# Band mask as a TensorE matmul, 18-token rows, a mode-contiguous spectrum and a pinned TensorE order in an attention and spectral-mix kernel

## Chip, cores and metric

The kernel runs on one core of a Trainium2 chip. The metric is the device time of one execution in microseconds, the median of several. The profile is of one execution; its times are counted from that execution's start.

## The reference

Eight batches of 576 tokens, 8 heads of 64. First comes attention in which a token sees itself and the 63 tokens before it; then a Fourier transform over the tokens, of which the first 64 modes are mixed, each by its own complex 512x512 matrix, transformed back and added; then one more matmul with a ReLU.

```python
def _attn_ref(q, k, v):                      # window = 64
    scores = scale * np.matmul(q, k.transpose(0, 1, 3, 2))
    rel = pos[:, None] - pos[None, :]
    scores = np.where((rel >= 0) & (rel < window), scores, -1e9)
    ...                                      # softmax over keys, times v
def _moe_ref(x, w_r, w_i, w_ch):
    X = np.fft.rfft(x, axis=1)               # first 64 modes, each with its own w_r, w_i (512x512)
    Yr = einsum('bmd,mde->bme', Xr, w_r) - einsum('bmd,mde->bme', Xi, w_i)
    Yi = einsum('bmd,mde->bme', Xr, w_i) + einsum('bmd,mde->bme', Xi, w_r)
    u = x + np.fft.irfft(Y, n=S, axis=1)
    return u + np.maximum(u @ w_ch, 0.0)
```

## The kernel before

The kernel has three stages. In stage 1, q, k and v of a batch are loaded and brought into place by TensorE (transposes of q and k, "pick" matmuls for v); attention then goes through 36 windows of 8 blocks of 64 tokens per head pair; the forward transform of each finished batch fills `XQ`. In stage 2 the 128 weight matrices (64 modes, real and imaginary) stream in and are multiplied with `XQ`. Stage 3 transforms back and writes the result. The program is written in an order, but where nothing else is said, a scheduler in the kernel language places the instructions of each engine.

These are the parts that the change touches (cuts marked `...`):

```python
RUN = S // 64                                            # 9 tokens per partition row
XQ = keep.tile([128, NC, NM, B, 3], BF16, name="XQ")     # mode outside, batch and part inside
ps_misc = ...tile_pool(name="ps_misc", bufs=2, space=PSUM)   # 2 buffers: transposes, v, transform
...
def main(src, dst, quad):                                # 4 such pieces per batch, 8 of 9 tokens
    def f():
        ps = ps_misc.tile([128, 8, 128], BF16, name="pst", tag="misc")
        for c in range(8):
            tr(src, quad, c, ps[:, c, :])
        evac(view(dst, quad * 2 * S, [[S, 2], [RUN, 64], [1, 8]]), view(ps, ...), 1024)
def last():                                              # the 9th token of each row, q and k
    ps = ps_misc.tile([128, 4, 128], BF16, name="psl", tag="misc")
    ...
    evac(view(dst, 8, [[S, 4], [RUN, 64]]), view(ps, ...), 256)     # single elements, 9 apart
def vpart(a, j0, j1):
    ...
    for c in range(4):
        for i in range(2):                               # two row groups, two PSUM tiles
            nc.tensor.matmul(out=pss[i][:, 0:n, :], lhsT=pick[pp, c, :], rhs=rv[pp, j0:j1, c, :], ...)
...
def scores(w):
    ...                                                  # 64x64 matmuls into pss[w % 2]
    nc.scalar.activation(out=et, in_=ps, func=ACT_F.Exp, scale=EX_SCALE)
    nc.vector.tensor_tensor(out=et, in0=et, in1=view(band, ...), op=ALU.mult)   # the band mask, 0 or 1
def weigh(w):
    for hh in range(2):
        for G in range(8 * w, 8 * w + 8):
            n, i = divmod(G, 9)                          # head, block of the head
            nc.tensor.matmul(out=pso[hh][...], lhsT=et[...], rhs=vt[...], start=True, stop=True)
            if i == 8:                                   # the head is complete: normalise it
                nc.vector.reciprocal(out=rcp, in_=view(pso[hh], D, ...))
                nc.vector.tensor_tensor(out=x_sb[...], in0=view(pso[hh], ...), in1=view(rcp, ...), op=ALU.mult)
def dft(b):
    ...
    nc.vector.tensor_copy(out=view(XQ, 3 * b + 1, [[NM * W3, NC], [1, 2], [W3, NM]]), in_=ps)
    nc.scalar.mul(out=view(XQ, 3 * b, [[NM * W3, NC], [W3, NM]]), in_=ps[:, :, 1, :], mul=-1.0)
...
for w in range(NWIN):                                    # 36 windows
    scores(w)
    for b, j in sched.get(w, []): units[b][j]()          # pieces of the next batch
    while dfts: dft(dfts.pop(0))
    if w: weigh(w - 1)
```

Note `pso[hh]`: each half `hh` has one PSUM buffer. The first block of the next head may write it only when the normalisation of the head before has read it.

The softmax here doesn't subtract the row's maximum and nothing guards it: scores larger than these inputs give would overflow.

## Time and profile before

| | kernel before |
|---|---|
| median time | 559.99 us (558.45 to 560.14) |
| stage 1, to the first spectral matmul | 216.7 us |
| stage 2, to the first inverse transform | 282.3 us |
| stage 3 | 60.0 us |

The first fence is the page's overview in 40 slices of 14 us: TensorE's busy tenths, the granted clock, the share of DMA and its GB/s.

```profile
PE   2988999988989777887888721222222222248882
...
PEclk9999999995665555799888855555555555559998
DMA  9999798979910020999999999999999999944554
GB/s 148 203 155 156 123 153 130 172 114 152 165 35 2 1 76 6 203 213 214 213 214 214 213 213 214 213 214 213 214 213 214 213 214 213 214 100 159 179 194 145
```

From slice 16 to 34 DMA runs at 203 to 214 GB/s, while TensorE, after some other work up to slice 22, is 10 to 20% busy: stage 2 is bounded by the weights. Just before it, slices 11 to 15, DMA is all but idle (the 76 GB/s of slice 14 are one other load), because every weight buffer is full and none comes free until stage 2 starts. So whatever shortens stage 1 shortens the whole.

Stage 1 in stretches of 20 us (window; then busy us and count for PE, PEld, DVE, ACT, POOL; granted clock; DMA share; GB/s):

```profile
60.00:80.00 20.00, 18.83 (x207) 11.36 (x206) 10.61 (x20) 10.63 (x14) 4.82 (x8) 1.00 0.86 131
80.00:100.00 20.00, 19.35 (x237) 12.40 (x235) 10.70 (x24) 12.23 (x14) 5.75 (x9) 1.00 0.91 144
100.00:120.00 20.00, 19.22 (x230) 12.12 (x229) 10.52 (x23) 10.27 (x14) 4.44 (x7) 1.00 0.78 133
160.00:180.00 20.00, 19.55 (x209) 11.70 (x207) 9.87 (x24) 9.30 (x14) 0.00 (x0) 0.50 0.00 1
```

TensorE is 94 to 98% busy in these stretches and about 80% in most others from 120 us on, so stage 1 is mainly TensorE's. The clock of 1.00 in the first three lines is not to be believed. The trace's first clock record is at 120 us, and the view takes full clock before it. The transforms tell otherwise: the chain of waits shows one of them at 79 us, 20 matmuls in 3.12 us, and within it the full-array matmuls of 128 columns start 107 ns apart; so they do at 58 and at 103 us. In a stretch of stage 2 where full clock is on record, 128-column transposes start 56 ns apart. Those are the two states, 1.2 and 2.4 GHz, of the Trainium skill, "TensorE: Matmul & The Clock Gate", Part 1. By this reading and the records from 120 us on, stage 1 ran at half clock except for 10 us of its 217.

The chain of waits at that transform (start, us, what):

```profile
79.11 3.12 PE psx L312 x20
82.26 2.50 DVE XQ L315
84.80 1.35 ACT XQ L316
```

The two copies into `XQ` follow one another and take 3.85 us together, and for that long they hold one of the two `ps_misc` buffers through which all pieces of the next batch pass.

The groups of stage 1 that the change touches (line, engine, operation, operands, shapes, count | busy us, mean ns | idle before, releaser):

```profile
L276 DVE TENSOR_TENSOR et<-et,band 128x1024 bf16<-128x1024 bf16 x36 | 24.8, 688 | 19.7 <-ACT et L274 19.6
...
L315 DVE CAST XQ<-psx 128x512 bf16<-128x512 f32 x8 | 20.0, 2504 | 16.9 <-PE psx L312 16.9
...
L316 ACT ACTIVATE XQ<-psx 128x256 bf16<-128x256 f32 x8 | 10.7, 1343 | 27.6 <-DVE XQ L315 16.1 <-DVE rcp L298 11.6
...
L62 ACT COPY qT<-pst 128x1024 bf16<-128x1024 bf16 x12 | 12.6, 1046 | 4.3 <-PE pst L206 3.9 <-PE pso_148 L291 0.4
L62 ACT COPY qT<-psl 128x256 bf16<-128x256 bf16 x5 | 7.8, 1564 | 1.5 <-DVE kT_142 L64 1.5
```

TensorE's waits for the normalisation, in stage 1 (who waited for whom: us, times, longest):

```profile
PE pso_148 L291 <- DVE x_sb L299: 4.3, 6, 1.5
...
PE pso_147 L291 <- DVE x_sb L299: 0.7, 1, 0.7
```

They are few: the scheduler puts other work between two heads.

### The profile page before, as it was taken

What the parts mean: (1) busy time and instruction counts of PE and PEld (TensorE: products, weight loads), DVE (VectorE), ACT (ScalarE), POOL (GpSimd) and SP (SyncE); (2) the same over time, 40 slices, a digit from 0 to 9 for tenths busy, and PEclk for the clock granted to TensorE, in tenths of its full rate; (3) what the DMA queues carried; (4) which work ended last, traced back from release to release, by engine and by line L of the source; (5) the groups of instructions that cost most, each with busy time, mean ns of one, the idle gap of its engine ahead of it and who ended that gap; (6) DMA issues with size and microseconds to landing.
All of it is one profiled execution on the core that took longest, in us unless ns stands there. A gap on an engine that the chain in (4) does not pass through costs nothing.

```text
span 559.0 us, 10870 instructions
## 1 busy us (share of the span) xinstructions
PE 354.5 (63%) x4760; PEld 242.7 (43%) x4760; DVE 188.8 (34%) x372; ACT 161.6 (29%) x226; POOL 156.5 (28%) x235
## 2 busy tenths in 40 slices
PE   2988999988989777887888721222222222248882
PEld 1655566555546546654555521222221222236551
DVE  4585555455545675523222200000000000016662
ACT  3468447553734622222222200000000000005552
POOL 8312133121300001312222212222122222009996
PEclk9999999995665555799888855555555555559998
DMA  9999798979910020999999999999999999944554
GB/s 148 203 155 156 123 153 130 172 114 152 165 35 2 1 76 6 203 213 214 213 214 214 213 213 214 213 214 213 214 213 214 213 214 213 214 100 159 179 194 145
DMA packets 42431, 92.45 MB, mean 165 GB/s; under 512 B 3472, under 2 KB 20880, under 8 KB 42384
## 3 DMA queue, kind: packets, MB, share of 16 engines
q0 software_dynamic: 37136, 82.32, 78.4%
q1 hardware_dynamic: 5248, 9.44, 4.8%
q8 instruction: 37, 0.61, 0.4%
q14 instruction: 10, 0.08, 0.0%
HBM read 163.58 MB, written 9.44 MB: 310 GB/s over the span
## 4 chain that ended last, share of the span: by engine, by line
DMA 40%; PE 24%; issue 16%; DVE 8%; POOL 6%; ACT 5%; POOLq 0%; DVEq 0%; ACTq 0%
DMA wt<-in_moe_w_r_dram 36%; POOL ot L478 5%; PE pst L206 4%; PE psx L312 3%; DMA wt<-in_moe_w_i_dram 3%; DVE XQ L315 3%; PE pso_148 L291 2%; PE pso_147 L291 2%; DVE u L474 2%; DMA rq<-in_q_dram 1%; PE pss_149 L269 1%; ACT qT L62 1%; ACT XQ L316 1%; PE pss_150 L269 1%; DVE qT L64 1%
## 5 line engine op out<-in xcount | busy, mean ns | idle before, releaser
L405 PE MATMUL psy<-XQ,wt 128*128 128x16 bf16 x1024 | 57.1, 174 | 86.6 <-DMA wt<-in_moe_w_i_dram 86.2
L402 PE MATMUL psy<-XQ,wt 128*128 128x16 bf16 x1024 | 59.6, 174 | 66.9 <-DMA wt<-in_moe_w_r_dram 63.4
L113 POOL DMA_DIRECT2D wt<-in_moe_w_r_dram x64 | 34.4, 538 | 222.8 <-PE psy L405 216.9
L405 PEld LDWEIGHTS <-wt 128*128 128x128 bf16 x1024 | 46.3, 102 | 92.9 <-DMA wt<-in_moe_w_i_dram 92.6
L402 PEld LDWEIGHTS <-wt 128*128 128x128 bf16 x1024 | 46.5, 103 | 79.4 <-DMA wt<-in_moe_w_r_dram 74.2
L408 DVE CAST YT<-psy 128x512 fp32r<-128x512 f32 x8 | 5.5, 691 | 180.5 <-PE psy L405 180.5
L478 POOL TENSOR_TENSOR ot<-u,r 128x512 f32<-128x512 f32 (+1 forms) x40 | 49.7, 1297 | 24.3 <-ACT r L476 24.3
L388 PE MATMUL psz<-wch,xT 128*128 128x512 f32 (+1 forms) x160 | 55.4, 472 | 1.8 <-DVE xT L385 1.4
L463 ACT CAST Yw<-psw_5958 128x512 fp32r<-128x512 f32 x1 | 0.6, 587 | 180.1 <-PE psw_5958 L458 180.1
L385 DVE CAST xT<-pxt 128x512 fp32r<-128x512 bf16 (+1 forms) x40 | 23.9, 632 | 65.9 <-PE pxt L382 65.9
L291 PEld LDWEIGHTS <-et 128*64 128x64 bf16 (+1 forms) x576 | 32.1, 146 | 31.6 <-issue 26.0
L390 ACT CAST Z_3076<-psz 128x512 fp32r<-128x512 f32 (+1 forms) x40 | 23.2, 583 | 70.3 <-PE psz L388 70.3
L113 POOL DMA_DIRECT2D wt<-in_moe_w_i_dram x64 | 35.1, 549 | 0.5 <-issue 0.5
L235 PEld LDWEIGHTS <-pick 32*128 32x128 bf16 x256 | 23.0, 121 | 25.9 <-issue 13.6
L388 PEld LDWEIGHTS psz<-wch,xT 128*128 128x128 f32 (+1 forms) x160 | 30.0, 209 | 7.7 <-ACT Z_3076 L390 2.4
L474 DVE TENSOR_TENSOR u<-psu,x_sb 128x512 f32<-128x512 f32 (+1 forms) x40 | 26.8, 688 | 19.5 <-POOL ot L478 13.3
L276 DVE TENSOR_TENSOR et<-et,band 128x1024 bf16<-128x1024 bf16 x36 | 24.8, 688 | 19.7 <-ACT et L274 19.6
L102 POOL DMA_DIRECT2D rv<-in_v_dram x32 | 19.5, 622 | 35.4 <-PE pss_149 L269 7.6
L476 ACT ACTIVATE r<-psc 128x512 f32<-128x512 f32 (+1 forms) x40 | 22.1, 598 | 22.8 <-PE psc L471 14.0
L315 DVE CAST XQ<-psx 128x512 bf16<-128x512 f32 x8 | 20.0, 2504 | 16.9 <-PE psx L312 16.9
L312 PE MATMUL psx<-trigF,x_sb 128*128 128x128 bf16 (+1 forms) x160 | 25.1, 303 | 0.0
L274 ACT ACTIVATE et<-pss_149 128x1024 bf16<-128x1024 f32 x18 | 19.5, 1081 | 14.0 <-PE pss_149 L269 13.2
(249 smaller groups left out, 613.4 us busy)
## 6 DMA issues: line engine op xcount, KB each, us to landing
wt<-in_moe_w_r_dram POOLq DMA_DIRECT2D x64, 512.0 KB, 16.1
wt<-in_moe_w_i_dram POOLq DMA_DIRECT2D x64, 512.0 KB, 18.0
out_dram<-ot SPq DMA_DIRECT2D x32, 256.0 KB, 2.0
rk<-in_k_dram POOLq DMA_DIRECT2D x8, 576.0 KB, 6.5
rq<-in_q_dram POOLq DMA_DIRECT2D x8, 576.0 KB, 7.4
rv<-in_v_dram POOLq DMA_DIRECT2D x32, 144.0 KB, 5.0
wch<-in_moe_w_ch_dram POOLq DMA_DIRECT2D x1, 1024.0 KB, 5.5
out_dram<-ot SPq DMA_DIRECT2D x8, 128.0 KB, 2.2
```

The costliest lines, as they stand in the source:

```text
L113: nc.gpsimd.dma_start(out=wt, in_=src[m].rearrange("(p c) e -> p c e", c=NC))
L276: nc.vector.tensor_tensor(out=et, in0=et, in1=view(band, 0, [[0, 2 * WIN // 128], [1, 128]]), op=ALU.mult)
L291: nc.tensor.matmul(out=pso[hh][po, (i // 2) * (D + 1):(i // 2 + 1) * (D + 1)], lhsT=et[pk, hh, col:col + 64], rhs=vt[pk, 1 - f % 2, 2 * qu ...
L312: nc.tensor.matmul(out=ps[:, c, :, :], lhsT=x_sb[:n, b, t, c:DM:NC], rhs=trigF[:n, t, :], start=(t == 0), stop=(t == NT - 1))
L315: nc.vector.tensor_copy(out=view(XQ, 3 * b + 1, [[NM * W3, NC], [1, 2], [W3, NM]]), in_=ps)
L385: nc.vector.tensor_copy(out=xT[:, :, 0:n], in_=pst[:, :, 0:n])
L388: nc.tensor.matmul(out=psz[:n, :], lhsT=xT[:, c, 0:n], rhs=wch[:, c, :], start=(c == 0), stop=(c == NC - 1))
L390: nc.scalar.copy(out=Z0[:n, b, t, :], in_=psz[:n, :])
L402: nc.tensor.matmul(out=psy[:, m % MG, e, :], lhsT=wr[:, c, ee], rhs=XQ[:, c, m, :, 1:3], start=(c == 0), stop=False)
L405: nc.tensor.matmul(out=psy[:, m % MG, e, :], lhsT=wi[:, c, ee], rhs=XQ[:, c, m, :, 0:2], start=False, stop=(c == NC - 1))
L474: nc.vector.tensor_tensor(out=u[:n, :], in0=psu[:n, :], in1=x_sb[:n, b, t, :], op=ALU.add)
L478: nc.gpsimd.tensor_tensor(out=ot[:n, :], in0=u[:n, :], in1=r[:n, :], op=ALU.add)
```

## The change

The intent is to take the mask off VectorE, to give TensorE more and wider work so that its clock rises, and to fix its order. The mask becomes a matmul: the identity times a band of 0 and -30000 opens the PSUM accumulation of each window, and the scores are added to it. Rows of 18 tokens per partition make six even transposing pieces per batch (3 for q, 3 for k), without the leftover. `XQ` gets the mode innermost, so its copies write contiguously. 24 warm-up matmuls go ahead. TensorE's instructions run in the order in which the program emits them, and the weighting of a window is cut into its two halves with pieces of the next batch between.

```diff
-    RUN = S // 64
+    RUN = S // 32
-    XQ = keep.tile([128, NC, NM, B, 3], BF16, name="XQ")
+    XQ = keep.tile([128, NC, B, 3, NM], BF16, name="XQ")
...
-        def main(src, dst, quad):  ...   # 8 chunks into PSUM, one copy of 1024
-        def last():  ...                 # the 9th token, two copies of 256, one for k and one for q
+        def part(src, dst, c0):
+            def f():
+                ps = ps_misc.tile([128, 6, 128], BF16, name="pst", tag="misc")
+                for c in range(6):
+                    for hh in range(2):
+                        nc.tensor.transpose(out=ps[64 * hh:64 * hh + 64, c, :], ...)
+                evac(view(dst, c0, [[S, 4], [RUN, 32], [1, 6]]), view(ps, ...), 768)
...
     def scores(w):
         ps = pss[w % 2]
+        for hh in range(2):
+            nc.tensor.matmul(out=ps[:, hh, :], lhsT=ident_bf, rhs=view(band, 0, [[0, WIN // 128], [1, 128]]),
+                             start=True, stop=False, skip_group_check=True)
...
-                                     start=True, stop=True, skip_group_check=True)
+                                     start=False, stop=True, skip_group_check=True)
-        nc.vector.tensor_tensor(out=et, in0=et, in1=view(band, ...), op=ALU.mult)
...
-    def weigh(w):
+    def weigh(w, hh):
...
-        nc.vector.tensor_copy(out=view(XQ, 3 * b + 1, [[NM * W3, NC], [1, 2], [W3, NM]]), in_=ps)
+        nc.vector.tensor_copy(out=view(XQ, b * 3 * NM + NM, [[BN, NC], [1, 2 * NM]]), in_=...)
...
+    with tc.manual_schedule(engines={mybir.EngineType.PE}):
+        warm_up(16)
...
+        for w in range(NWIN + 1):
+            todo = list(sched.get(w, []))
+            if w < NWIN: scores(w)
+            if todo: unit(*todo.pop(0))
+            if w: weigh(w - 1, 0)
+            if todo: unit(*todo.pop(0))
+            if w: weigh(w - 1, 1)
...
```

More of the change, by code (lines that the diff above doesn't have):

```diff
@@ L93, in load @@
     def load(b):
-        rk = rawp.tile([128, 4, RUN * D], BF16, name="rk")
-        rq = rawp.tile([128, 4, RUN * D], BF16, name="rq")
+        rk = rawp.tile([128, 2, RUN * D], BF16, name="rk")
+        rq = rawp.tile([128, 2, RUN * D], BF16, name="rq")
         rv = rawp.tile([128, 9, 4, D], BF16, name="rv")
@@ L98, in load @@
             nc.gpsimd.dma_start(
-                out=r, in_=src[b].rearrange("(x g) (p c) d -> (g p) x (c d)", g=2, c=RUN))
+                out=r, in_=src[b].rearrange("(x g) (p c) d -> (g p) x (c d)", g=4, c=RUN))
         vf = v[b].rearrange("(hp hl) t d -> hp (hl t) d", hl=2)
@@ L114, in load_w @@
         wtiles[i] = wt
+    warm = acons.tile([128, 512], BF16, name="warm")
+    nc.vector.memset(warm, 0.0)
     load(0)
@@ L130 @@
                                 base=0, pattern=[[-1, 4], [1, 128]], channel_multiplier=-4)
+    NEG = -30000.0
     band = acons.tile([128, 128], BF16, name="band")
-    nc.vector.memset(band, 1.0)
+    nc.vector.memset(band, 0.0)
     for half in range(2):
@@ L138 @@
         nxt_ = band[pp, 64 - 64 * half:128 - 64 * half]
-        nc.gpsimd.affine_select(out=own, in_=own, compare_op=ALU.is_ge, fill=0.0,
+        nc.gpsimd.affine_select(out=own, in_=own, compare_op=ALU.is_ge, fill=NEG,
                                 base=0, pattern=[[1, 64]], channel_multiplier=-1)
-        nc.gpsimd.affine_select(out=nxt_, in_=nxt_, compare_op=ALU.is_ge, fill=0.0,
+        nc.gpsimd.affine_select(out=nxt_, in_=nxt_, compare_op=ALU.is_ge, fill=NEG,
                                 base=-1, pattern=[[-1, 64]], channel_multiplier=1)
     load(1)
-    kTs = [acons.tile([128, 2, 2, S], BF16, name=f"kT{i}") for i in range(2)]
+    kTs = [acons.tile([128, 4, S], BF16, name=f"kT{i}") for i in range(2)]
     vts = [acons.tile([128, 2, 4, 9, D + 1], BF16, name=f"vt{i}") for i in range(2)]
@@ L154 @@
         nc.vector.memset(pso[i], 1.0)
-        nc.vector.memset(pss[i], 0.0)
     MAGIC = 12582912.0
@@ L199, in transpose_units @@
         rq, rk, rv = raws[b]
-        qT = qtp.tile([128, 2, 2, S], BF16, name="qT")
+        qT = qtp.tile([128, 4, S], BF16, name="qT")
         kT, vt = kTs[b % 2], vts[b % 2]
         qTs[b] = qT
-        def tr(src, quad, c, dst):
-            for hh in range(2):
-                nc.tensor.transpose(out=dst[64 * hh:64 * hh + 64, :],
-                                    in_=src[:, 2 * quad + hh, c * D:(c + 1) * D], identity=ident_bf)
-        def main(src, dst, quad):
-            def f():
-                ps = ps_misc.tile([128, 8, 128], BF16, name="pst", tag="misc")
-                for c in range(8):
-                    tr(src, quad, c, ps[:, c, :])
-                evac(view(dst, quad * 2 * S, [[S, 2], [RUN, 64], [1, 8]]),
-                     view(ps, 0, [[64, 2], [1, 64], [128, 8]]), 1024)
-            return f
-        def last():
-            ps = ps_misc.tile([128, 4, 128], BF16, name="psl", tag="misc")
-            for i, src in enumerate((rk, rq)):
-                for quad in range(2):
-                    tr(src, quad, 8, ps[:, 2 * i + quad, :])
-            for i, dst in enumerate((kT, qT)):
-                evac(view(dst, 8, [[S, 4], [RUN, 64]]),
-                     view(ps, 256 * i, [[64, 4], [1, 64]]), 256)
+        def part(src, dst, c0):
+            def f():
+                ps = ps_misc.tile([128, 6, 128], BF16, name="pst", tag="misc")
+                for c in range(6):
+                    for hh in range(2):
+                        nc.tensor.transpose(out=ps[64 * hh:64 * hh + 64, c, :],
+                                            in_=src[:, hh, (c0 + c) * D:(c0 + c + 1) * D],
+                                            identity=ident_bf)
+                evac(view(dst, c0, [[S, 4], [RUN, 32], [1, 6]]),
+                     view(ps, 0, [[32, 4], [1, 32], [128, 6]]), 768)
+            return f
         def vpart(a, j0, j1):
@@ L245, in vpart @@
             return f
-        return [main(rk, kT, 0), main(rq, qT, 0), last, vpart(0, 0, 5), vpart(0, 5, 9),
-                main(rk, kT, 1), main(rq, qT, 1), vpart(1, 0, 5), vpart(1, 5, 9)]
+        return [part(rk, kT, 0), part(rk, kT, 6), part(rk, kT, 12),
+                part(rq, qT, 0), part(rq, qT, 6), part(rq, qT, 12),
+                vpart(0, 0, 5), vpart(0, 5, 9), vpart(1, 0, 5), vpart(1, 5, 9)]
     def head_of(n):
-        return n // 4, n % 4 // 2, n % 2
+        return n // 4, n % 4
     def scores(w):
         ps = pss[w % 2]
+        for hh in range(2):
+            nc.tensor.matmul(out=ps[:, hh, :], lhsT=ident_bf, rhs=view(band, 0, [[0, WIN // 128], [1, 128]]),
+                             start=True, stop=False, skip_group_check=True)
         for G in range(8 * w, 8 * w + 8):
             n, blk = divmod(G, 9)
-            b, quad, g = head_of(n)
+            b, g = head_of(n)
             first = G == 8 * w
@@ L269, in scores @@
                     nc.tensor.matmul(out=ps[64 * half:64 * half + 64, hh, col:col + nq],
-                                     lhsT=kTs[b % 2][pp, quad, g, 64 * kb:64 * kb + 64],
-                                     rhs=qTs[b][pp, quad, g, q0:q0 + nq],
-                                     start=True, stop=True, skip_group_check=True)
+                                     lhsT=kTs[b % 2][pp, g, 64 * kb:64 * kb + 64],
+                                     rhs=qTs[b][pp, g, q0:q0 + nq],
+                                     start=False, stop=True, skip_group_check=True)
         et = etp.tile([128, 2, WIN], BF16, name="et")
@@ L275, in scores @@
         busy["ACT"] += 2 * WIN / 1.2 + 60
-        nc.vector.tensor_tensor(out=et, in0=et, in1=view(band, 0, [[0, 2 * WIN // 128], [1, 128]]), op=ALU.mult)
-        busy["DVE"] += 2 * WIN / 1.92 + 70
         ets[w] = et
-    def weigh(w):
-        et = ets.pop(w)
-        for hh in range(2):
-            for G in range(8 * w, 8 * w + 8):
-                n, i = divmod(G, 9)
-                b, quad, g = head_of(n)
-                vt = vts[b % 2]
-                f = G % 18
-                po = slice(64 * (i % 2), 64 * (i % 2) + 64)
-                col = 64 * (G - 8 * w)
-                pk = slice(0, 128) if i else slice(64 * (f % 2), 64 * (f % 2) + 64)
-                nc.tensor.matmul(out=pso[hh][po, (i // 2) * (D + 1):(i // 2 + 1) * (D + 1)],
-                                 lhsT=et[pk, hh, col:col + 64], rhs=vt[pk, 1 - f % 2, 2 * quad + hh, f // 2, :],
-                                 start=True, stop=True, skip_group_check=True)
-                if i == 8:
-                    ps = pso[hh]
-                    h = 4 * quad + 2 * hh + g
-                    rcp = small.tile([128, NT], FP32, name="rcp")
-                    nc.vector.reciprocal(out=rcp, in_=view(ps, D, [[D + 1, NT]]))
-                    nc.vector.tensor_tensor(
-                        out=x_sb[:, b, :, h * D:(h + 1) * D],
-                        in0=view(ps, 0, [[D + 1, NT], [1, D]]),
-                        in1=view(rcp, 0, [[1, NT], [0, D]]), op=ALU.mult)
-                    busy["DVE"] += NT * D / 0.96 + 150
-                    if h == H - 1:
-                        dfts.append(b)
@@ new lines, in weigh @@
+    def weigh(w, hh):
+        et = ets[w]
+        for G in range(8 * w, 8 * w + 8):
+            n, i = divmod(G, 9)
+            b, g = head_of(n)
+            vt = vts[b % 2]
+            f = G % 18
+            po = slice(64 * (i % 2), 64 * (i % 2) + 64)
+            col = 64 * (G - 8 * w)
+            pk = slice(0, 128) if i else slice(64 * (f % 2), 64 * (f % 2) + 64)
+            nc.tensor.matmul(out=pso[hh][po, (i // 2) * (D + 1):(i // 2 + 1) * (D + 1)],
+                             lhsT=et[pk, hh, col:col + 64], rhs=vt[pk, 1 - f % 2, 2 * hh + g // 2, f // 2, :],
+                             start=True, stop=True, skip_group_check=True)
+            if i == 8:
+                ps = pso[hh]
+                h = 4 * hh + g
+                rcp = small.tile([128, NT], FP32, name="rcp")
+                nc.vector.reciprocal(out=rcp, in_=view(ps, D, [[D + 1, NT]]))
+                nc.vector.tensor_tensor(
+                    out=x_sb[:, b, :, h * D:(h + 1) * D],
+                    in0=view(ps, 0, [[D + 1, NT], [1, D]]),
+                    in1=view(rcp, 0, [[1, NT], [0, D]]), op=ALU.mult)
+                busy["DVE"] += NT * D / 0.96 + 200
+                if h == H - 1:
+                    dfts.append(b)
@@ L313, in dft @@
                                  rhs=trigF[:n, t, :], start=(t == 0), stop=(t == NT - 1))
-        W3 = 3 * B
-        nc.vector.tensor_copy(out=view(XQ, 3 * b + 1, [[NM * W3, NC], [1, 2], [W3, NM]]), in_=ps)
-        nc.scalar.mul(out=view(XQ, 3 * b, [[NM * W3, NC], [W3, NM]]), in_=ps[:, :, 1, :], mul=-1.0)
+        BN = B * 3 * NM
+        nc.vector.tensor_copy(out=view(XQ, b * 3 * NM + NM, [[BN, NC], [1, 2 * NM]]), in_=ps.rearrange("p c r m -> p c (r m)"))
+        nc.scalar.mul(out=view(XQ, b * 3 * NM, [[BN, NC], [1, NM]]), in_=ps[:, :, 1, :], mul=-1.0)
         busy["DVE"] += 600
@@ L328, in early, with warm_up, unit @@
                 nw += 1
+    def warm_up(n):
+        ps = ps_misc.tile([128, 512], FP32, name="psd", tag="misc")
+        for _ in range(n):
+            nc.tensor.matmul(out=ps, lhsT=warm[:, 0:128], rhs=warm, start=True, stop=True)
     dfts = []
     NWIN = B * H * S // (2 * WIN)
-    for u in transpose_units(0):
-        u()
-    load(2)
-    early(2)
-    sched = {}
-    PB = NWIN / B
-    for b in range(1, B):
-        for j in range(9):
-            sched.setdefault(int(PB * (b - 1) + j * PB / 10), []).append((b, j))
-    units = {}
-    for w in range(NWIN):
-        scores(w)
-        for b, j in sched.get(w, []):
+    PB = NWIN / B
+    with tc.manual_schedule(engines={mybir.EngineType.PE}):
+        warm_up(16)
+        for i, u in enumerate(transpose_units(0)):
+            u()
+            if i in (2, 5):
+                warm_up(4)
+        load(2)
+        early(2)
+        NU = 10
+        sched = {}
+        for b in range(1, B):
+            for j in range(NU):
+                sched.setdefault(int(PB * (b - 1) + j * PB / (NU + 1)), []).append((b, j))
+        units = {}
+        def unit(b, j):
             if j == 0:
@@ L347 @@
             units[b][j]()
-            if j == 8:
+            if j == NU - 1:
                 if b + 2 < B:
@@ L351 @@
                 early(3)
-        while dfts:
-            dft(dfts.pop(0))
-        if w:
-            weigh(w - 1)
-    early(EARLY)
-    weigh(NWIN - 1)
-    while dfts:
-        dft(dfts.pop(0))
+        for w in range(NWIN + 1):
+            todo = list(sched.get(w, []))
+            if w < NWIN:
+                scores(w)
+            if todo:
+                unit(*todo.pop(0))
+            if w:
+                weigh(w - 1, 0)
+            if todo:
+                unit(*todo.pop(0))
+            if w:
+                weigh(w - 1, 1)
+            while todo:
+                unit(*todo.pop(0))
+            while dfts:
+                dft(dfts.pop(0))
+        early(EARLY)
     p1.close()
@@ L402 @@
                     nc.tensor.matmul(out=psy[:, m % MG, e, :], lhsT=wr[:, c, ee],
-                                     rhs=XQ[:, c, m, :, 1:3], start=(c == 0), stop=False)
+                                     rhs=XQ[:, c, :, 1:3, m], start=(c == 0), stop=False)
                 for c in range(NC):
                     nc.tensor.matmul(out=psy[:, m % MG, e, :], lhsT=wi[:, c, ee],
-                                     rhs=XQ[:, c, m, :, 0:2], start=False, stop=(c == NC - 1))
+                                     rhs=XQ[:, c, :, 0:2, m], start=False, stop=(c == NC - 1))
             if m % MG == MG - 1:
```

## The prediction

> **What bounds it now.** Three stages (page, timeline, windows). (1) Attention and forward transform, 0 to 216.7 us, when the first spectral matmul starts. (2) Spectral mix to about 498 us: DMA share 1.06 at 213 GB/s, PE busy only in bursts; DMA bounds it. (3) Inverse transform and output, about 60 us. Only stage 1 and XQ's layout change. DMA is idle from about 154 to 222 us because the weight slots are full, so each microsecond off stage 1 should come off the total.
>
> Stage 1 is PE's: windows from 60 to 120 us show it 94-97% busy. It runs cold. The page prints a clock of 1.0 up to 120 us, but the transform's 128-column matmuls start 107 ns apart there; in a later stretch granted full clock, 128-column transposes start 56 ns apart. That is the 1.2 against 2.4 GHz of the Trainium skill, "TensorE: Matmul & The Clock Gate", Part 1; the first clock record only comes at 120 us. By the records, the clock rises after a 3.4 us slot with about 73% array work and falls after one below about 39%.
>
> **Removed.** 36 band multiplies on DVE (688 ns each, 24.8 us; mostly slack). XQ's strided writes: DVE 2.50 -> about 0.7 us, ACT 1.34 -> about 0.4 us per batch; only the last pair is on the path, about 3 us. Larger q/k rows: hidden DMA.
>
> **Added.** Two 512-column matmuls per window: 72 x 427 ns = 31 us cold, 72 x 216 = 15.5 us warm, all on PE. Warm-ups hide behind the first load.
>
> **Moved.** In emission order the paired V matmuls alternate row groups and overlap (8 in about 1.0 us where serial quartets take 0.96-1.2 us each): about -2.5 us per batch; fewer tiling switches (a switch after scores costs about 244 ns start to start; "TensorEngine Tiling", Key Properties, says a mode change drains, and the trace agrees). Against that, 56 head boundaries inside a half-window now leave PE waiting for reciprocal (0.2 us) and normalisation (0.49 us), about 0.87 us with semaphores, which the old order filled: about +6 us per batch.
>
> **Sum per batch** (my estimates from these durations; before takes 21.6 us from transform to transform). All warm: mask 2.4, scores 1.8, weighting with its waits 10.1, transposes 2.6, V 2.4, transform 2.0 = 21.3; with a first window at 18 us in place of the old eager prologue (first transform only at 58 us), stage 1 is about 183 us, total 526. All cold: 30.3 per batch, stage 1 about 254, total 597. So the clock decides. Array work in the warm sum is about 36% of the time, just under where the clock fell before; but mask and warm-ups exist to hold it. I lean to mostly warm.
>
> **Prediction: 532 us, 8 in 10 within 505 to 588.** Faster 0.68, same 0.12, slower 0.20.
>
> **What would show it.** Stage 1 ending near 185-190 us; transform cadence near 56 ns, mask matmuls near 216 ns apart; PE waits on normalisation of about 0.9 us, 56 times; XQ copies under 0.8 us; DVE busy down about 35 us; stages 2 and 3 still 343 us together.
>
> **What would make it wrong.** The clock dropping to half for most of stage 1 (mask matmuls 427 ns apart, total near 590); later loads landing late behind weights issued ahead of them; evacuations on ACT holding PE; or strided XQ reads slowing stage 2's matmuls beyond a mode's 4.9 us of weights.

## The result

| | before | after |
|---|---|---|
| median time | 559.91 us | 593.28 us |
| stage 1 | 216.7 us | 247.3 us |
| stage 2 | 282.3 us | 283.9 us |
| stage 3 | 60.0 us | 58.1 us |
| full clock in stage 1 | 10 us | 48 us |

The changed kernel is slower: the ratio is 1.0598, with a 95% interval of 1.056 to 1.0636. A ratio here is the mean time of one kernel's fast runs over the mean time of the other's fast runs of the same rounds, so it is not quite the ratio of the medians. The whole difference lies in stage 1.

The overview of the changed kernel, same lines as above:

```profile
PE   7777687767767767897877762222222222228884
...
PEclk9855575557555855579899995555555555558998
DMA  9999999226500000279999999999999999982554
GB/s 155 204 215 210 210 207 170 41 41 85 78 1 2 1 1 1 73 145 215 212 213 214 214 214 214 214 214 213 213 213 214 213 214 214 214 161 93 191 190 170
```

The slack of DMA before stage 2 has grown (slices 7 to 16), as stage 1 takes longer. TensorE's own line has fallen from nines to sevens. The clock now has records from the start: half for most of stage 1.

The same stretches as before:

```profile
60.00:80.00 20.00, 15.36 (x183) 8.36 (x183) 6.38 (x18) 7.29 (x12) 5.62 (x10) 0.50 1.09 209
80.00:100.00 20.00, 15.44 (x211) 8.13 (x211) 7.84 (x17) 6.37 (x12) 5.63 (x10) 0.67 1.05 192
100.00:120.00 20.00, 13.67 (x184) 9.44 (x178) 6.54 (x15) 6.48 (x8) 1.44 (x2) 0.50 0.36 53
160.00:180.00 20.00, 13.88 (x173) 9.05 (x172) 6.37 (x15) 5.61 (x8) 0.34 (x2) 0.50 0.09 12
```

VectorE and ScalarE have less to do (6 to 8 us of 20, where they had 9 to 12), but TensorE is down to 68 to 77% busy: it waits. For what is shown by its waits over stage 1:

```profile
PE pso_157 L284 <- DVE x_sb L292: 33.6, 28, 2.2
PE pso_158 L284 <- DVE x_sb L292: 24.7, 27, 1.5
```

58.3 us in 55 waits, where the kernel before had 5.0 us. One of them, from the timeline around 101 us (start, us, engine, line, what):

```profile
100.68 0.32 PE L284 MATMUL pso_157<-vt_153,et 128*64 128x65 bf16 x3
101.03 0.20 DVE L291 RECIPROCAL rcp<-pso_157 128x5 f32<-128x5 f32 x1 [2.09 <-PE pso_157 L284]
...
101.26 0.49 DVE L292 TENSOR_TENSOR x_sb<-pso_157,rcp 128x320 bf16<-128x320 f32 x1
101.81 0.47 PE L284 MATMUL pso_157<-vt_153,et 64*64 64x65 bf16 x5 [0.81 <-DVE x_sb L292]
```

The third matmul of the first line completes a head. TensorE's next matmul begins the next head in the same PSUM buffer. It has to wait for the reciprocal and the multiplication on VectorE, and starts 0.81 us after the previous one has ended. Transposes, scores and v matmuls stand ready behind it, but matmuls run in program order (the Trainium skill, "TensorE: Matmul & The Clock Gate", Part 3, "What overlaps and what doesn't", says it; the trace agrees, as no matmul starts in the 0.81 us).

The groups that answer to those of before:

```profile
L250 PE MATMUL pss_160<-band,ident_bf 128*128 128x512 bf16 x36 | 17.3, 581 | 0.0
L250 PE MATMUL pss_159<-band,ident_bf 128*128 128x512 bf16 x36 | 16.5, 555 | 0.0
...
L62 ACT COPY qT<-pst 128x768 bf16<-128x768 bf16 x10 | 8.1, 811 | 10.9 <-PE pst L212 5.8 <-PE pso_158 L284 4.9
...
L308 DVE CAST XQ<-psx 128x512 bf16<-128x512 f32 x8 | 5.5, 692 | 23.7 <-PE psx L305 23.7
...
L309 ACT ACTIVATE XQ<-psx 128x256 bf16<-128x256 f32 x8 | 3.1, 384 | 33.0 <-DVE XQ L308 33.0
```

The mask matmuls came out about as costed at half clock: in 28 of the 36 pairs the second starts some 401 ns after the first (in the other 8 some 226), and all 72 take 31.3 us from start to start. The copies into `XQ` fell as forecast, to 0.69 and 0.38 us.

An account of stage 1 from the trace: the time from each matmul's start to the next one's start, summed by kind, so a wait counts with the matmul before it.

```
us in stage 1    transposes    v    mask  scores  weighting  transform  warm-ups
before                 41.3  58.9       -    32.1       45.6       24.5         -
after                  29.7  33.0    31.3    18.5      100.4       22.3       7.9
```

The mask adds 31.3 us and the weighting 54.8 us. Transposes, v and scores give back 51 us together. The rest is small. So two suspects stand: the order's waits and the mask's matmuls; and behind both the clock.

### The profile page after: what moved, and what is told of

It is laid out like the page before. It is cut to its first block, busy times and chain, and to the rows that moved or that the text cites. A ratio compares the mean times of both kernels' runs of the same rounds, so it can differ in the third digit from the quotient of the medians.

```text
span 589.3 us, 11010 instructions
## 1 busy us (share of the span) xinstructions
PE 356.7 (61%) x4856; PEld 233.7 (40%) x4856; DVE 161.3 (27%) x341; ACT 138.4 (23%) x220; POOL 155.8 (26%) x235
## 4 chain that ended last, share of the span: by engine, by line
DMA 38%; PE 29%; DVE 13%; issue 13%; POOL 5%; ACT 1%; POOLq 0%; DVEq 0%
DMA wt<-in_moe_w_r_dram 28%; DMA wt<-in_moe_w_i_dram 9%; DVE x_sb L292 5%; PE pst L212 5%; POOL ot L490 4%; PE psx L305 3%; PE pso_158 L284 3%; PE pss_160 L250 3%; PE pso_157 L284 3%; PE pss_159 L250 2%; DVE u L486 2%; DVE qT L64 2%; DVE rcp L291 2%; PE pss_160 L265 2%; PE pss_159 L265 1%
## 5 line engine op out<-in xcount | busy, mean ns | idle before, releaser
L417 PE MATMUL psy<-XQ,wt 128*128 128x16 bf16 x1024 | 62.5, 191 | 90.7 <-DMA wt<-in_moe_w_i_dram 90.4
L414 PE MATMUL psy<-XQ,wt 128*128 128x16 bf16 x1024 | 65.1, 191 | 60.0 <-DMA wt<-in_moe_w_r_dram 59.7
L417 PEld LDWEIGHTS <-wt 128*128 128x128 bf16 x1024 | 48.3, 104 | 98.1 <-DMA wt<-in_moe_w_i_dram 97.9
L414 PEld LDWEIGHTS <-wt 128*128 128x128 bf16 x1024 | 48.5, 104 | 72.6 <-DMA wt<-in_moe_w_r_dram 71.7
L284 PEld LDWEIGHTS <-et 128*64 128x64 bf16 (+1 forms) x576 | 33.4, 142 | 74.6 <-issue 69.3
L400 PE MATMUL psz<-wch,xT 128*128 128x512 f32 (+1 forms) x160 | 49.6, 431 | 1.8 <-DVE xT L397 1.4
L400 PEld LDWEIGHTS psz<-wch,xT 128*128 128x128 f32 (+1 forms) x160 | 27.2, 190 | 6.9 <-ACT Z_3158 L402 2.4
L270 ACT ACTIVATE et<-pss_160 128x1024 bf16<-128x1024 f32 x18 | 18.4, 1023 | 27.7 <-PE pss_160 L265 27.7
L270 ACT ACTIVATE et<-pss_159 128x1024 bf16<-128x1024 f32 x18 | 18.4, 1022 | 27.5 <-PE pss_159 L265 27.5
L284 PE MATMUL pso_157<-vt_154,et 128*64 128x65 bf16 (+1 forms) x144 | 12.4, 248 | 19.2 <-DVE x_sb L292 19.2
L305 PE MATMUL psx<-trigF,x_sb 128*128 128x128 bf16 (+1 forms) x160 | 22.8, 282 | 1.3 <-DVE x_sb L292 1.3
```

The lines of the kernel that those rows point to most:

```text
L284: nc.tensor.matmul(out=pso[hh][po, (i // 2) * (D + 1):(i // 2 + 1) * (D + 1)], lhsT=et[pk, hh, col:col + 64], rhs=vt[pk, 1 - f % 2, 2 * hh ...
L305: nc.tensor.matmul(out=ps[:, c, :, :], lhsT=x_sb[:n, b, t, c:DM:NC], rhs=trigF[:n, t, :], start=(t == 0), stop=(t == NT - 1))
L400: nc.tensor.matmul(out=psz[:n, :], lhsT=xT[:, c, 0:n], rhs=wch[:, c, :], start=(c == 0), stop=(c == NC - 1))
L414: nc.tensor.matmul(out=psy[:, m % MG, e, :], lhsT=wr[:, c, ee], rhs=XQ[:, c, :, 1:3, m], start=(c == 0), stop=False)
L417: nc.tensor.matmul(out=psy[:, m % MG, e, :], lhsT=wi[:, c, ee], rhs=XQ[:, c, :, 0:2, m], start=False, stop=(c == NC - 1))
```

## The experiments

All are built from the changed kernel by undoing or moving single parts, except that one starts from the kernel before. "First run", "fifth run" and so on follow the numbers in the labels (e1 is the first). Every kernel gave the right result, and each was timed in three rounds against the kernel before. The table has all of them; the details follow. Medians are of fast runs. Of e5's four runs (505.1, 507.7, 512.2 and 521.5 us) the last was slow, over 1.5% above the fastest; with it the median is 509.9, and that is the 510 us which the later texts take for the fifth run.

```
label                      median us  ratio to before (95%)     stage 1  full clock  order      mask     rows  XQ
before                        560.5   -                          216.7        5%     scheduler  VectorE  old   old
after                         593.3   1.0598 (1.056-1.0636)      247.3       19%     pinned     TensorE  new   new
e1_list_order                 520.0   0.9275 (0.9227-0.9323)     175.4       57%     scheduler  TensorE  new   new
e2_dve_mask                   574.7   1.0268 (1.0241-1.0294)     231.7        9%     pinned     VectorE  new   new
e3_split                      539.2   0.9629 (0.9596-0.9662)     193.9       46%     pinned, split  TensorE  new  new
e4_split_dve_mask             538.9   0.9597 (0.9548-0.9645)     196.9        5%     pinned, split  VectorE  new  new
e5_list_dve_mask              507.7   0.9075 (0.9017-0.9134)     164.3       42%     scheduler  VectorE  new   new
e6_list_dve_mask_filler       525.5   0.9379 (0.9354-0.9404)     180.9       49%     scheduler  VectorE + filler  new  new
e7_list_no_warm_up            522.5   0.9314 (0.9284-0.9345)     178.2       46%     scheduler  TensorE  new   new
e8_mask_in_wait               564.7   1.0089 (1.0056-1.0123)     220.9       25%     pinned     TensorE  new   new
e9_before_xq                  544.8   0.9732 (0.9694-0.977)      200.2        7%     scheduler  VectorE  old   new
e10_e5_old_xq                 534.6   0.9546 (0.9501-0.9592)     190.0       27%     scheduler  VectorE  new   old
e11_e5_old_loop               510.3   0.9113 (0.9092-0.9134)     167.4       33%     scheduler  VectorE  new   new
e12_rows_only                 527.8   0.9425 (0.9405-0.9446)     184.0       24%     scheduler  VectorE  new   old
```

"Full clock" is the share of stage 1 that the records grant full clock, with half clock before the first record. In all 14 profiles the span less stage 1 is between 341.4 and 344.1 us, so every difference is one of stage 1.

### Order and mask apart

**e1: the emission order undone.**

```diff
-    with tc.manual_schedule(engines={mybir.EngineType.PE}):
+    with ExitStack():
```

> The changed kernel with TensorE's emission order undone (the scheduler places TensorE again); mask, rows, XQ layout and warm-ups stay. Theory A (the 58 us of TensorE waits for normalisation at head boundaries, made by the pinned order, are the largest cost): those waits nearly vanish (under 15 us in all), but the V matmuls fall back to serial quartets (about +20 us) and the mask's 31 us stay, so the total is 575 to 590 us. Theory B (the mask's 31 us on a cold TensorE are the loss, the order is worth nothing): within 1% of 593.

Measured: 520.0 us, 73 us below the changed kernel and 7% below the kernel before. TensorE's waits for the normalisation:

```profile
PE pso L284 <- DVE x_sb L292: 1.3, 3, 0.7
```

The direction is theory A's, but the size is outside what either theory had written. The order costs not 3 to 18 us but 73, and the rest of the change gains. Theory B as it stood (the order is worth nothing) is out. Also, the v matmuls took 35 us in all, near the 33 under the pinned order, but at a higher clock. At half clock one took 163 ns on average from start to start here, 132 in the changed kernel and 226 in the kernel before, so part of their overlap was lost.

**e2: the mask back on VectorE, the order kept.**

```diff
...
-        for hh in range(2):
-            nc.tensor.matmul(out=ps[:, hh, :], lhsT=ident_bf, rhs=view(band, ...), start=True, stop=False, ...)
...
+        nc.vector.tensor_tensor(out=et, in0=et, in1=view(band, ...), op=ALU.mult)
```

> The changed kernel with the mask back on VectorE as a multiply after exp; the emission order, rows, XQ layout and warm-ups stay. Theory B: 593 less 31 us of mask matmuls and about 4 us of tiling switches, so 555 to 560 us, the time of before. Theory A: the same 31 us come off but the waits remain and may lengthen (VectorE has 25 us more), so 560 to 570 us, and TensorE still waits 55 us or more on normalisation.

Measured: 574.7 us, above both ranges: 19 us come off, not the 23 to 38 that the two had. The waits are 59.7 us in 55, as theory A had it. What the wide matmuls had given is gone: full clock falls from 19% of stage 1 to 9%. Transposes now take 35.6 us against 29.7, v 35.9 against 33.0. So the mask on TensorE costs 19 us here, against the 73 of the order in e1.

**e3: the order kept, other work put where TensorE waited.** Each window's weighting is cut at the head boundary, and the next window's scores and pieces go between.

```diff
-    def weigh(w, hh):
+    def weigh(w, hh, late):
...
+            if late != (n > 8 * w // 9):     # n is the head: before or after the boundary
+                continue
...
+            if w:
+                weigh(w - 1, 0, False); weigh(w - 1, 1, False)
             if w < NWIN:
                 scores(w)
+            while todo:
+                unit(*todo.pop(0))
+            if w:
+                weigh(w - 1, 0, True); weigh(w - 1, 1, True)
```

> The changed kernel, still in emission order with the mask on TensorE, but each window's weighting cut at the head boundary: the part before it of both halves, then the next window's scores and the pieces of transposes and V, then the part after it. Nothing is taken away, only other work is put where TensorE waited. Theory A: waits on normalisation fall from 58 us to under 10 us and the total to 535 to 550 us if the clock stays cold; if the denser array also lifts the clock above half for most of the first stage, 490 to 520 us. Theory B: waits only move, 580 us or more.

Measured: 539.2 us, 54 us below the changed kernel, with the same matmuls, in another pinned order. Of the waits for the normalisation one of 0.2 us is left. The largest that remain are these:

```profile
PE psv L227 <- ACT qT L62: 9.9, 8, 2.5
PE pso L286 <- ACT et L270: 5.7, 8, 1.8
PE psv L227 <- ACT vt L62: 4.0, 7, 0.9
```

The first and third come from my putting all pieces of a window in one place, so that they queue for the two `ps_misc` buffers; the second is a wait for the exponential of the window. Theory A holds. Full clock rose to 46% of stage 1, but the time came down no further than the all-cold range: there are 25 us of new waits, and transposes and v together take 20 us more from start to start than in the changed kernel.

**e4: both.** Diff: those of e2 and e3 together.

> As the previous one with the mask back on VectorE. Theory A: the costs add up, so about 35 us under the previous one if both are cold: 500 to 515 us. If the wide mask matmul is what keeps the clock up (theory C), this one falls behind the previous one or equals it, because its array work per 3.4 us slot is smaller by about a quarter.

Measured: 538.9 us, the same as e3. The costs do not add up, which is what theory C had said. The stretches of e3 show why (same columns as above):

```profile
60.00:100.00 40.00, 35.64 (x559) 22.07 (x562) 18.47 (x47) 18.43 (x30) 11.67 (x19) 0.76 1.13 210
100.00:140.00 40.00, 35.70 (x522) 21.26 (x518) 18.10 (x46) 18.03 (x29) 7.07 (x12) 0.71 0.59 91
140.00:180.00 40.00, 33.72 (x501) 19.22 (x500) 18.25 (x49) 16.53 (x27) 0.00 (x0) 0.76 0.01 2
```

and those of e4:

```profile
60.00:100.00 40.00, 35.56 (x500) 24.12 (x499) 19.59 (x48) 19.98 (x30) 11.91 (x20) 0.50 1.05 188
100.00:140.00 40.00, 36.36 (x510) 24.19 (x514) 20.25 (x50) 19.68 (x31) 7.34 (x13) 0.50 0.70 114
140.00:180.00 40.00, 34.33 (x480) 22.03 (x481) 21.19 (x54) 19.90 (x32) 0.00 (x0) 0.50 0.01 2
```

With the wide matmuls the clock is 0.71 to 0.76, without them 0.50. From start to start in stage 1, e3 pays 27.4 us for the mask. It spends 30 us less on everything else together (transposes 36.0 against 43.3, v 47.1 against 51.2, scores 16.1 against 22.4, weighting 36.9 against 43.6, transform with the first transposes of stage 2 21.2 against 26.8, warm-ups 8.0 against 8.4). TensorE's waits in stage 1 do not tell the two apart (25 us in e3, 24 in e4). The mask matmul pays for itself through the clock, and that is all it does: the medians are the same.

**e8: the mask moved into the waits.**

```diff
...
+                if G < 8 * w + 7 and w + 2 < NWIN:
+                    mask(w + 2, hh)      # right after the head's last matmul; its PSUM tile is free by then
```

> The changed kernel in its emission order, with the mask matmul of a later window's half issued at the head boundary, where TensorE waits for the normalisation; same matmuls, same waits, other place. Theory A: the mask's 31 us hide in the waits (56 of the 72 matmuls), 565 to 572 us if the clock stays cold; by theory C the denser array may lift it, then 535 to 560 us. Theory B, that the wide matmul as such costs: 590 us.

Measured: 564.7 us, 29 us below the changed kernel, at the lower edge of the cold range. The waits have shrunk by the same amount:

```profile
PE pso L291 <- DVE x_sb L299: 29.7, 55, 1.6
```

Full clock rose only from 19% to 25% of stage 1. So about half of the 58 us of waits is shown here to be lost TensorE time that other matmuls can have for nothing, which a cost of the matmuls as such (theory B) would not allow.

### Where the gain of e1 came from

Theory C, after these runs, was that e1 is fast because the wide matmuls raise the clock. Its rival D was that the rows, the `XQ` layout or the warm-ups gain.

**e5: scheduler order and mask on VectorE.** Diff: those of e1 and e2.

> Scheduler order and mask on VectorE: of the change only the 18-token rows, the XQ layout and the warm-ups are left. If the gain of the first run (520 us) comes from the wide matmuls lifting TensorE's clock (theory C), this one stays cold (clock near 0.5 in the first stage, transforms 107 ns apart) and takes 548 to 560 us. If it comes from the rows, the XQ layout or the warm-ups (theory D), it is at 530 us or less.

Measured: 507.7 us (505.1 to 512.2 in the three fast runs), the fastest of all. Theory C is wrong as the cause of the gain, and D is right: the mask on TensorE costs 12 us here (e1 against e5). The clock rose without any wide matmul after the warm-ups:

```profile
60.00:100.00 40.00, 39.62 (x601) 27.24 (x600) 23.45 (x56) 23.64 (x37) 11.68 (x19) 0.68 1.05 185
100.00:140.00 40.00, 38.74 (x625) 26.42 (x619) 25.09 (x61) 25.46 (x41) 6.19 (x11) 0.83 0.68 124
```

**e6: the wide matmuls as filler.** The two matmuls per window stay but the scores overwrite them; the mask is VectorE's.

```diff
+        for hh in range(2):
+            nc.tensor.matmul(out=ps[:, hh, :], lhsT=ident_bf, rhs=view(band, ...), start=True, stop=True, ...)
```

> As the previous one, with the two wide matmuls per window kept as pure filler: they write the scores' PSUM tile, and the scores overwrite it; the mask is VectorE's. 72 matmuls of work that no result needs. Theory C: the clock rises as in the first run and the total falls below the previous one, to 515 to 535 us. If instead the first run gained by taking the mask off VectorE (theory E), the filler costs its 31 us cold and this one takes 575 to 590 us.

Measured: 525.5 us. This is inside the range written for theory C, but that theory also asked for less than e5, and it is 18 us more. Against e1 the filler differs only in who masks: taking the mask off VectorE is worth 5 us. The filler's 28 us of matmuls cost 18 us net; the rest presumably came back through the higher clock (49% full against 42%).

**e7: no warm-ups.** From e1, the 24 warm-up matmuls removed.

> The first run (scheduler order, mask on TensorE) without the 24 warm-up matmuls. If the wide mask matmuls alone lift and hold the clock, within 1.5% of the first run, 517 to 528 us; the first 30 us may be cold. If the clock has to be lifted at the start and is then only held, the first stage is cold and the total 575 us or more.

Measured: 522.5 us, 2.5 us above e1, on the first alternative; the intervals of the two ratios overlap. The warm-ups are nearly free and worth little; nothing has to be lifted at the start to be held.

### Rows or spectrum layout

**e9: the kernel before with the new `XQ` layout alone.** Diff: the three `XQ` lines of the change.

> The kernel before with only the XQ layout of the change. Its copies out of PSUM (VectorE 2.50 us, ScalarE 1.34 us, one after the other) fall to about 0.69 and 0.39 us. Theory F (the slow XQ copies hold one of two PSUM buffers nearly 4 us per batch, and that starves TensorE and its clock): 525 to 540 us. Theory G (the 18-token rows with their three even parts are what gained in the fifth run): only the last copy counts, 554 to 558 us.

Measured: 544.8 us, 16 us below before, between the two ranges: more than only the last copy, less than theory F's. TensorE's waits for the `XQ` copies in stage 1, 8.1 us in the kernel before (11.6 us in e12, 8.0 in e10, the two others with the old layout), are gone. The two longest in the kernel before, and the one of e12, were these:

```profile
PE pst L206 <- ACT XQ L316: 4.2, 2, 2.2
PE psv_2361 L235 <- ACT XQ L316: 2.7, 1, 2.7
```

```profile
PE psv L226 <- ACT XQ L307: 11.6, 6, 3.1
```

The clock stayed where it was (7% full), so the gain here is not the clock's. The waits are half of it, and the last pair of copies, now 1.1 us in place of 3.9, gives some 3 us more; the rest is not taken apart.

**e10: e5 with the old `XQ` layout.** Diff: the same lines, reversed.

> The fifth run (scheduler order, mask on VectorE, 510 us) with the old XQ layout. Theory F: the gain goes, 540 us or more. Theory G: 513 to 522 us.

Measured: 534.6 us, 27 us above e5, again between the ranges. Full clock falls from 42% to 27%.

**e11: e5 with the window loop of before.** The order in which the program emits scores, pieces, transform and weighting is that of before.

> The fifth run with the window loop of before (scores, then all pieces, then transform, then both halves of the weighting). Under F and G alike the scheduler places the instructions, so within 2% of the fifth run; more than 15 us above it if the order in which the program emits them is what the scheduler needs (theory H).

Measured: 510.3 us, within 1% of e5. Theory H is out: the scheduler does not need the new loop.

**e12: the rows alone.** The kernel before with 18-token rows and the ten even pieces; nothing else.

> The kernel before with only the 18-token rows (and the ten even pieces per batch that they bring): old XQ layout, old loop, no warm-ups, mask on VectorE, scheduler order. Theory G: 515 to 530 us. Theory F: 550 us or more. With the run of XQ alone it says whether the two parts add up.

Measured: 527.8 us, 33 us below before. Theory G has the larger half and F the smaller, and the two parts add up: 33 and 16 us make 511 us, where e11 measured 510. Of the rows' part this much is shown. The 256-element copies are gone, and what is left are copies like these:

```profile
L62 ACT COPY qT<-pst 128x768 bf16<-128x768 bf16 x17 | 13.4, 825 | 4.3 <-PE pst L211 3.5 <-PE pso L282 0.8
```

All copies of transposes together took 56.0 us before and 41.0 us in this run, and the v matmuls 58.9 and 48.0 us from start to start. Full clock rose from 5% to 24%. How much of the 33 us is the copies, how much the more even pieces and how much the longer DMA rows was not taken apart, and stays open.

### The clock, from all profiles

For each 3.4 us slot between two possible clock changes in stage 1 I summed the array work, that is columns times the used share of the array, over the granted clock, as a share of the slot. (The records last multiples of 3.41 us.) It is my estimate, from the matmuls in the traces. All 14 profiles together, 806 slots:

```
slot at half clock:  work share   below .60   .60-.70   .70-.80   above .80
                     slots             404       118        56          13
                     next at full        1        19        42          13
slot at full clock:  work share   below .30   .30-.40   above .40
                     slots              52        45         118
                     next at full        0        23         118
```

In these profiles the clock rose after about 70% work and was held by 40%; between 30 and 40% it stayed in about half of the slots. The rule that the prediction took from a single profile (73 and 39) was about right.

## Why the prediction was wrong

The forecast was 532 us, in 505 to 588; measured were 593. Point by point:

- **What bounds the kernel** was right: stage 1, on TensorE, at half clock, with stages 2 and 3 unchanged (342.0 us together, forecast about 343). Every run moved by what stage 1 moved.
- **The head-boundary waits** were right in kind and count and a little small: 55 waits of 1.06 us on average (58.3 us), forecast 56 of about 0.87. Undoing the order took 73 us off (e1); putting work there took 54 off (e3), with the clock's rise in both.
- **The mask at half clock** was right: 31.3 us against 31 (8 of the 36 pairs at full clock, and what follows each pair counted in).
- **The step that failed is "I lean to mostly warm".** Stage 1 was granted full clock for 19% of its time. The prediction had the deciding comparison in hand, array work of about 36% against the 39% under which the clock fell, and set it aside because the mask and the warm-ups "exist to hold it". The pooled table bears the comparison out: of the full-clock slots below 40% work, 23 of 97 stayed; above 40%, all did. Nor did the average speak for the clock coming back: at half clock the same matmuls fill about 51% of the 30.3 us forecast for a batch (my estimate: 36% of 21.3 us, doubled), and of the 404 half-clock slots below 60% one was followed by full clock. The sum for "all cold", 597 us, was within 1% of the measurement, which is partly luck: the waits were 10 us longer than forecast, 48 us of stage 1 were not cold, and the two pull in opposite directions. An intent that can be read off the code is no evidence that it works.
- **Why the clock fell** is, as far as shown, the waits: with the waits filled and the same matmuls (e3), full clock held for 46% of stage 1; with the scheduler's order (e1), 57%.
- **"Larger q/k rows: hidden DMA" and "only the last pair is on the path, about 3 us"** were both mis-sized. The rows are worth 33 us (e12), the layout 16 us (e9) to 27 us (e10 against e5). Both were costed as work taken off engines with slack. For the layout, TensorE's waits on the held PSUM buffer show part of it (8 to 12 us with the old layout, none with the new); for the rows the like is only argued. These two errors did not spoil the sum for "all cold", which was built from the new kernel's own matmuls; but they hid that most of the change gains and one part of it loses more.
- **The v matmuls** did overlap as forecast: eight in 1.03 or 1.25 us at half clock, where a quartet of the kernel before took up to 1.24. The pinned order had a part in it: at half clock a v matmul takes 132 ns from start to start, against 163 in e1 and 186 in e5. What the scheduler loses there it makes up by the clock (35.1 us in e1 against 33.0 in all).

So the change joins two parts that gain (rows 33 us, layout 16), one that gains nothing (the mask: 12 us lost under the scheduler, 0 in e3, 19 lost as shipped) and one that loses 67 to 73 us (the pinned order: e2 against e5, after against e1). Without order and mask it takes 508 us, 9% less than before.

## What to carry to other kernels

When an engine's order is pinned, look for each place where it waits for another engine in the middle of a run of its own work; here the scheduler filled all but 1.3 of the 58 us (e1), and the pinned order paid each in full, and the clock on top. A slow copy out of PSUM on an engine with slack is not free if it holds one of two buffers through which the bottleneck passes. Adding array work to lift the clock can pay for itself, but here it never paid more: take waits out first.

## What the Trainium skill lacked or had wrong

- "TensorE: Matmul & The Clock Gate", "Why this matters for your kernels", asks for no idle gaps above about 3 us between bursts to stay at full clock. Here the clock fell after every one of 52 full-clock slots with under 30% array work, though in 27 of them no stretch without a streaming matmul reached 1 us (for instance the slot at 85.9 us of e5: 29% work, longest such stretch 0.14 us). All 118 slots above 40% held. A share of array work in the slot describes it; the longest gap does not.
- The same page, Part 4, says that full clock does not engage for PE transposes, as they do not count as busy the same way. In some 20 slots of these profiles transposes made up 50% or more of the slot at half clock, and the clock rose after them; the slot at 140.7 us of the kernel before had 75% work, of which transposes were 54 points, so only 21% without them. And transposes at full clock started 56 ns apart. (The trace lists them as matmuls with the identity; it does not show whether they ran in the transpose mode that the page means.)
- No page that I found says that a clock view has no value before the first clock record. In the kernel before it read 1.00 for 120 us in which 128-column matmuls started 107 ns apart.
- "SBUF — State Buffer" warns of a penalty for each access to a new 16-byte line, but no page that I found gives a figure for a copy out of PSUM with single 2-byte elements on the output side: 256 of them at a step of 9 elements took 1.28 to 1.56 us (means by group), 768 in runs of 6 took 0.81 us on ScalarE.
